# First key weights over ScalarE's DMA queue, centred first and last tiles, row scales on ScalarE, and new orders in a four-layer attention kernel

## The chip, the cores and the metric

The kernel runs on one core of one Trainium2 chip. The metric is the device time of one execution in microseconds, given as the median of several runs. The profile shows one execution: PE is TensorE, DVE is VectorE, ACT is ScalarE, POOL is GpSimd, SP is SyncE, which here issues DMAs only.

## The reference

Four layers follow each other on one sequence of 2048 tokens and 512 features, in 32 heads of 16: linear attention (A), sliding-window attention (B, a window of 256 keys), A and B again with the same weights. Each layer adds its result to x.

```python
phi = lambda t: jnp.where(t > 0, t + 1, jnp.exp(t)) + 1e-6
# A, on q, k, v of the normalised x
pq, pk = phi(q), phi(k)
kv = jnp.einsum("bhsd,bhse->bhde", pk, v)
z = jnp.einsum("bhsd->bhd", pk)
num = jnp.einsum("bhqd,bhde->bhqe", pq, kv)
den = jnp.einsum("bhqd,bhd->bhq", pq, z)[..., None] + 1e-6
o = num / den
# B
scores = jnp.einsum("bhqd,bhkd->bhqk", q, k) * (Dh ** -0.5)
mask = (idx[:, None] - idx[None, :] >= 0) & (idx[:, None] - idx[None, :] < W)
p = _softmax(jnp.where(mask[None, None], scores, -1e9), axis=-1)
o = jnp.einsum("bhqk,bhkd->bhqd", p, v)
# the model; _A_ref and _B_ref end with the product with wo
x = A_x
x = x + _A_ref(_layernorm(x, axis=-1), A_wqkv, A_wo)
x = x + _B_ref(_layernorm(x, axis=-1), B_wqkv, B_wo)
x = x + _A_ref(_layernorm(x, axis=-1), A_wqkv, A_wo)
x = x + _B_ref(_layernorm(x, axis=-1), B_wqkv, B_wo)
```

## The kernel before

The sequence is cut into 16 tiles of 128 tokens. All weights and activations stay in the core's memory in bf16.

**Layer one, keys.** For each tile VectorE takes the mean and variance (`stats` L377, `aggr` L378), a small addition and GpSimd's power give the reciprocal deviation `rs` (L382, L383), VectorE writes the normalised tile `xn` (L384). It is transposed: the first five tiles by PE (L398) with an eviction (L405), the rest by DMA transposes on SP (L392). From the transposed tile in `XQ` PE forms k (`tok`, L423) with the key weights `wA[:, :, 512:1024]`; `phi` turns k into the positive feature: ScalarE's exponential `E` (L447), VectorE's minimum `E1` (L450), then one of two forms. In the plain form VectorE takes the maximum with k + 1 straight from PSUM (`phi`, L454). In the other, called near in the code, ScalarE writes k + 1 (`R`, L449) and VectorE takes the maximum of two bf16 tiles (`mx`, L452). The Gram products `g` (L527) collect xnᵀ·phi(k) in four banks of PSUM over all tiles. The q of two tiles at a time (L483) goes through the same `phi`; `BY_ACT` lists the tiles of q that take the form with `R`.

**Barrier one.** From the Gram matrix follow kv and z (L542, L551), the matrix M = kv·wo (L581), the denominators (L597), their reciprocals (L606), their spread over features (L616) and the scaling of q (L626, L628). The layer's output is one product with M for each tile (`aout`, L423) and an addition to x (L641).

**Layer two** runs tile by tile: norm, transposes, q and k (`feat`, L437), v (`bv`, L423, evicted to `vS`, L410), small DMAs that lay keys and values out (L673, L692), scores (L713, L749, L829), exponentials on ScalarE (L723, L758, L838; 156 of them), masks (L731, L763, and on GpSimd L809), the product with v (L859), the division (L871, L872), the output product `bout` (L423), and x's update. The norm and the keys of layer three (`a_k`, `a_v`) follow for each tile; its key-value sums (L506) close **barrier two**, which is built like the first. **Layer four** repeats layer two with the output DMAs at its end (L915, L981).

**The start.** Nine matmuls on zeros (L1124) and up to seven fillers (`FILL`, L277) run on PE before the first data. SP issues x and the key weights in two halves in turn. ScalarE's queue issues one small DMA at the start (L1119) whose only reader is a wait ahead of the first layout DMA.

**What sets the order.** Nothing is decided at run time. The program makes a list of operations; `TABLE` is a packed table with a place in the order, an engine and a PSUM bank for each. `place` unpacks it, `synchronise` works out the semaphore waits, and each engine plays its own operations in that order. An operation that waits holds up all behind it on its engine. SP's DMAs use a ring of 48 semaphores.

## Time and profile before

| what | value |
| --- | --- |
| median of 3 runs | 410.35 us |
| lowest and highest run | 409.96 and 411.26 us |
| the profiled execution, its own time | 409.59 us |
| its span, first to last instruction | 407.9 us |
| granted TensorE clock, mean | 0.996 |
| PE busy | 395.0 us, 97% of the span |
| ACT busy | 350.4 us, 86% |
| DVE busy | 348.3 us, 85% |
| POOL busy | 130.3 us, 32% |
| bytes moved by DMA | 37.14 MB, 91 GB/s over the span |

A row of the timeline gives the start, the length, the engine, the line, what is written and what is read, how often the instruction comes in a row, and in brackets the idle time ahead of it with what ended it. A row of a window gives its length, then the busy time of each engine with the number of its instructions, the granted clock, the DMA engines' share and their rate. In the table of groups the last figure is the idle time ahead of the group's instructions.

### The profile page before, as it was taken

How to read it: one execution, taken by the hardware profiler on the slowest of the kernel's cores; microseconds unless marked ns; L12 is line 12 of the kernel's file. 1: busy time of each engine (PE TensorE's matmuls, PEld its weight loads, DVE VectorE, ACT ScalarE, POOL GpSimd, SP SyncE). 2: the span in 40 equal slices, each digit the busy share in tenths (PEclk: the TensorE clock that was granted, in tenths of full speed). 3: DMA queues.
4: the chain of work that ended last, by engine and by line, in shares of the span. 5: the costliest groups of instructions: out<-in, count | busy, mean ns of one | idle time of the engine just before them, and what ended most of it. 6: DMA issues, size and time to landing. Idle time of an engine off the chain costs nothing.

```text
span 407.9 us, 16954 instructions
## 1 busy us (share of the span) xinstructions
PE 395.0 (97%) x7402; PEld 255.8 (63%) x7402; DVE 348.3 (85%) x816; ACT 350.4 (86%) x444; POOL 130.3 (32%) x222
## 2 busy tenths in 40 slices
PE   8999999999999999999999999999999989999996
PEld 3744676677475567565657767576657746666674
DVE  6998899999998899888879789998998688766675
ACT  3743669999999998999997378999999999989991
POOL 4678562030342342431302132121116052303421
PEclk9999999999999999999999999999999999989999
DMA  7566015652264423363222101353315443342442
GB/s 242 113 163 192 4 29 132 160 106 56 60 115 81 121 68 96 88 113 82 70 64 33 27 2 28 83 121 95 80 29 133 74 129 91 97 123 55 123 94 69
DMA packets 66609, 37.14 MB, mean 91 GB/s; under 512 B 47656, under 2 KB 61864, under 8 KB 66536
## 3 DMA queue, kind: packets, MB, share of 16 engines
q1 hardware_dynamic: 66048, 34.75, 36.7%
q8 instruction: 58, 0.95, 1.0%
q0 software_dynamic: 480, 1.31, 0.9%
q14 instruction: 15, 0.12, 0.1%
q10 hardware_dynamic: 8, 0.00, 0.0%
HBM read 6.29 MB, written 2.10 MB: 21 GB/s over the span
## 4 chain that ended last, share of the span: by engine, by line
PE 65%; ACT 25%; DVE 7%; issue 1%; POOL 0%; POOLq 0%
PE ps L423 23%; ACT pb L723 15%; PE ps L859 12%; PE ps L437 10%; PE ps L713 6%; PE ps L483 5%; ACT pb L838 4%; ACT vp L723 4%; PE ps L527 3%; PE ps L829 1%; DVE xres L641 1%; DVE XQ L628 1%; DVE stats L377 1%; PE ps L1124 1%; PE ps L506 1%
## 5 line engine op out<-in xcount | busy, mean ns | idle before, releaser
L723 ACT ACTIVATE pb<-ps 128x1024 bf16<-128x1024 f32 (+2 forms) x216 | 199.8, 1022 | 8.4 <-PE ps L713 7.1
L859 PEld LDWEIGHTS ps<-vB,pb 128*128 128x128 bf16 x2560 | 79.0, 96 | 12.0 <-issue 2.7
L859 PE MATMUL ps<-vB,pb 128*128 128x34 bf16 x2560 | 84.9, 177 | 1.2 <-issue 0.5
L437 PE MATMUL ps<-xT,wBp 128*128 128x128 bf16 x1024 | 69.9, 221 | 0.6 <-ACT pb L723 0.5
L809 POOL TENSOR_SCALAR_AFFINE_SELECT pb<-pb 128x1024 bf16<-128x1024 bf16 x34 | 39.5, 1161 | 91.2 <-DVE pb L731 28.0
L437 PEld LDWEIGHTS ps<-xT,wBp 128*128 128x128 bf16 x1024 | 59.5, 98 | 12.8 <-issue 5.1
L382 POOL TENSOR_SCALAR ve<-mv 128x1 f32<-128x1 f32 x63 | 17.5, 278 | 154.5 <-DVE mv L378 152.9
L447 ACT ACTIVATE tE<-ps 128x512 bf16<-128x512 f32 x64 | 38.2, 606 | 20.6 <-PE ps L423 11.7
L713 PE MATMUL ps<-XQ,kB 32*128 32x256 bf16 (+3 forms) x992 | 48.2, 269 | 2.8 <-ACT vp L723 0.5
L423 PE MATMUL ps<-wA,XQ 128*128 128x512 bf16 x192 | 48.8, 379 | 0.0
L641 DVE TENSOR_TENSOR xres<-ps,xres 128x512 bf16<-128x512 f32 x63 | 42.8, 684 | 5.0 <-PE ps L423 4.9
L731 DVE TENSOR_TENSOR pb<-pb,tri 128x512 bf16<-128x512 bf16 (+1 forms) x108 | 43.1, 407 | 4.6 <-ACT pb L723 4.3
L377 DVE BATCH_NORM_STATS2 stats<-xres 128x6 f32<-128x512 bf16 x64 | 43.2, 684 | 2.5 <-DMA xres<-in_A_x_dram 2.1
L838 ACT ACTIVATE pb<-ps 128x1024 bf16<-128x1024 f32 x42 | 41.2, 1054 | 0.5 <-PE ps L829 0.4
L383 POOL TENSOR_TENSOR rs<-ve,negh 128x1 f32<-128x1 f32 x64 | 37.9, 592 | 7.8 <-DVE ve L380 2.5
L423 PE MATMUL ps<-wBv,xT 128*128 128x512 bf16 x128 | 34.4, 381 | 0.5 <-ACT pb L838 0.5
L483 PE MATMUL ps<-XQ,wA 128*128 128x256 bf16 x256 | 34.2, 273 | 0.4 <-ACT pb L723 0.4
L423 PE MATMUL ps<-M,XQ 128*128 128x512 bf16 x128 | 33.5, 380 | 0.4 <-DVE XQ L628 0.2
L423 PE MATMUL ps<-wBo,oT 128*128 128x512 bf16 x124 | 33.0, 380 | 0.4 <-ACT pb L723 0.3
L713 PEld LDWEIGHTS ps<-XQ,kB 32*128 32x128 bf16 x992 | 14.8, 92 | 28.3 <-ACT pb L723 7.3
L871 DVE RECIPROCAL rc<-ps 128x16 f32<-128x16 f32 x64 | 16.0, 252 | 14.8 <-PE ps L859 13.7
L483 PEld LDWEIGHTS ps<-XQ,wA 128*128 128x128 bf16 x256 | 23.4, 98 | 7.9 <-ACT pb L723 0.9
(133 smaller groups left out, 556.1 us busy)
## 6 DMA issues: line engine op xcount, KB each, us to landing
vB<-vS SPq DMA_DIRECT2D x64, 136.0 KB, 2.5
kB<-vp SPq DMA_DIRECT2D x60, 128.0 KB, 2.1
out_dram<-xres POOLq DMA_DIRECT2D x10, 128.0 KB, 2.4
wA<-in_A_wqkv_dram SPq DMA_DIRECT2D x2, 512.0 KB, 5.5
xres<-in_A_x_dram SPq DMA_DIRECT2D x2, 512.0 KB, 5.3
pb<-in_B_wqkv_dram SPq DMA_DIRECT2D x1, 1024.0 KB, 6.1
xres<-in_A_x_dram SPq DMA_DIRECT2D x3, 256.0 KB, 4.6
out_dram<-xres SPq DMA_DIRECT2D x5, 128.0 KB, 2.8
```

The costliest lines, as they stand in the source:

```text
L377: self.on("DVE", "stats", lambda e: e.bn_stats(K.stats[:, t, :], x()), key, dve(512), rd=rd, wr=[("stats", t)], **held)
L423: m = e.matmul(K.ps(ps), lhs(c), rhs(c), start=c == 0 and not whole, stop=c == 3)
L437: m = e.matmul(K.ps(ps)[:, f * P:(f + 1) * P], w(c, f), xT(c), start=c == 0, stop=c == 3)
L447: self.on("ACT", "E", lambda e: e.activation(K.tE[:, s, :], K.ps(ps), ACT.Exp, bias=0.0), key, act(512), wr=[("tE", s)], ps=[ps])
L483: m = e.matmul(K.ps(ps)[:, 256 * h:256 * h + 256], K.wA[:, c, f * P:(f + 1) * P], xT(c), start=c == 0, stop=c == 3)
L641: self.on("DVE", "res", lambda e: e.tensor_tensor(K.xres[:, t, :], K.ps(po), K.xres[:, t, :], ALU.add), key, dve(512), rd=[("xres", t)], w ...
L713: m = e.matmul(K.ps(ps[gq])[:, ns * i:ns * i + ns], K.kB[rows, j % 4, 2 * f + b, :, :], K.XQ[rows, f, q:q + ns], start=True, stop=True, ti ...
L723: return e.activation(out(2 * h, 2, ns), i, ACT.Exp, bias=0.0, scale=0.25)
L731: return e.tensor_tensor(x, x, K.tri[:, 0, sh:64].unsqueeze(1).unsqueeze(1).to_broadcast([P, 4, n, 64 - sh]), ALU.mult)
L809: return e.affine_select(out=x, in_=x, compare_op=ALU.is_ge, fill=0.0, base=-2, pattern=[[0, 16], [-2, 64]], channel_multiplier=1)
L838: return e.activation(far(h), i, ACT.Exp, bias=0.0, scale=0.25)
L859: m = e.matmul(K.ps(ps)[:, 34 * u:34 * u + 34], K.P((b // 2) % rp)[:, gq, f, o:o + P], K.vB[:, (b // 2) % 4, b % 2, r, :], start=i == 0, s ...
```

## The change

1. **Key weights.** ScalarE's queue loads the two halves of layer one's key weights as its first instructions, each with a semaphore of its own; the first two k products wait for these. SP no longer loads them, and the small DMA with its wait is gone.
2. **First two tiles centred.** For tiles 0 and 1 of layer one (`CENTRED`), ScalarE writes mean − x (`xc`, an Identity with scale −1 and the mean as its bias), PE transposes that in two halves, and the halves are evicted with a factor of −1 into `xT`. The k product reads this centred tile, and ScalarE's `E` and `R` take the row scale `rs` as their factor. The normalised tile is still written for the Gram matrix. Since PE no longer transposes it, a DMA transpose on SP brings it to `XQ` for the q product: 13 such transposes in layer one instead of 11.
3. **Keys with `R`.** The keys of tiles 0 to 7 of layer one (`KEYS_BY_ACT`) take the form with `R` and `mx`, and so do q tiles 7 to 10 of layer one's q (`BY_ACT`).
4. **Last tile of layer two.** Its output product is formed in halves, as the program's last tile is already; its norm is centred as in 2; k and v of layer three read the centred tile, with the row scale in `E`, `R` and in v's eviction.
5. **New table.** All orders, the choice of engine where there is one, and the banks. PE keeps its number of instructions; ScalarE has 472 operations instead of 447; GpSimd issues 6 output DMAs instead of 10 and SP 9 instead of 5.

```diff
-BY_ACT = {2: (0, 1, 2, 3, 4, 5, 6), 3: (4, 5, 6, 7, 8)}
+BY_ACT = {2: (0, 1, 2, 3, 4, 5, 6, 7, 8, 9, 10), 3: (4, 5, 6, 7, 8)}
+CENTRED = (0, 1)
+KEYS_BY_ACT = (0, 1, 2, 3, 4, 5, 6, 7)
...
-        seq += [xs(0, 1), wk(0), wk(1), xs(1, 2), w("wAq", "wA", "A_wqkv", 0, 512), xs(2, 4), xs(4, 6), xs(6, 8), xs(8, 12)]
+        seq += [xs(0, 1), xs(1, 2), w("wAq", "wA", "A_wqkv", 0, 512), xs(2, 4), xs(4, 6), xs(6, 8), xs(8, 12)]
...
+        if centred is not None:
+            slot, col = centred
+            self.on("ACT", "xc", lambda e: e.activation(K.xn[:, slot, :], x(), ACT.Identity, bias=K.mv[:, t, 0:1], scale=-1.0), key + 0.015, act(512), rd=rd + [("mv", t)], wr=[("xn", slot)])
+            for h in range(2):
+                half = Tile(1, K.cls)
...
+                        m = e.transpose(K.bf(half, 256)[:, c * P:(c + 1) * P], K.xn[:, slot, (2 * h + c) * P:(2 * h + c + 1) * P], K.ident[:])
...
+                self.either("Te", lambda e, eng, h=h, half=half: e.activation(K.xT[:, col, 2 * h:2 * h + 2, :], K.bf(half, 256).rearrange("p (c n) -> p c n", c=2), ACT.Copy, scale=-1.0) if eng == "ACT" else
...
+            by_pe = False
...
+        scale = lambda: dict(scale=K.rs[:, row, :]) if row is not None else {}
...
+        self.on("ACT", "E", lambda e: e.activation(K.tE[:, s, :], K.ps(ps), ACT.Exp, bias=0.0, **scale()), key, act(512), rd=own, wr=[("tE", s)], ps=[ps])
+        if near or row is not None:
+            self.on("ACT", "R", lambda e: e.activation(out(), view(K.ps(ps)), ACT.Identity, bias=K.one[:], **scale()), key + 0.005, act(512), rd=[("one",)] + own, wr=wr, ps=[ps], after=after)
...
-            po = self.b_out(j, k, tail, j in WHOLE[ph])
+            po = self.b_out(j, k, tail, j in WHOLE[ph], ph == 2 and j == T - 1)
...
+                end = j == T - 1
+                col = 1 if end else None
+                self.norm(j, k, 3, lambda j=j: K.XQ[:, :, j * P:(j + 1) * P], [("XQ", j)], tail and not end, po, near=end, centred=(1, 1) if end else None)
+                self.a_k(j, k + par["k_ak"], col)
...
-            tsem, touched = cx.enter_context(nc.semaphore("s_touch")), []
+            ksem, half = [cx.enter_context(nc.semaphore(f"s_key{h}")) for h in range(2)], []
...
-                    e.dma_start(self.kB[0:1, 3, 0:4, :, :].rearrange("p k n a -> p k (n a)"), self.A_wqkv.rearrange("(k p) c -> p k c", p=P)[0:1, :, 0:128]).then_inc(tsem, 16)
+                    for h in range(2):
+                        e.dma_start(self.wA[:, 2 * h:2 * h + 2, 512:1024], self.A_wqkv.rearrange("(k p) c -> p k c", p=P)[:, 2 * h:2 * h + 2, 512:1024]).then_inc(ksem[h], 16)
...
-                    if o.name == "kd" and not touched:
-                        touched.append(1)
-                        e.wait_ge(tsem, 16)
+                    if o.name == "k" and len(half) < 2:
+                        e.wait_ge(ksem[len(half)], 16)
+                        half.append(o)
```

What the table's new numbers do is seen in the engines' lists. PE at the start, before (a row is a line of the program, the operation, output and inputs, shape, and how often it comes in a row; `kB` holds the zeros of the warm matmuls and fillers, `vp` the normalised tiles, `ident` the identity of a transpose):

```order
L1124 MATMUL ps<-kB 128x512 x9
L277 MATMUL ps<-kB 128x512 x4
L398 MATMUL ps<-ident,vp 128x128 x4
L277 MATMUL ps<-kB 128x512
L398 MATMUL ps<-ident,vp 128x128 x4
L277 MATMUL ps<-kB 128x512
L423 MATMUL ps<-wA,XQ 128x512 x4
```

And with the change, where the line numbers have moved (L280 is the filler, L393 a half transpose of a centred tile, L439 the k product, L506 the q product):

```order
L1159 MATMUL ps<-kB 128x512 x9
L393 MATMUL ps<-ident,xn 128x128 x2
L280 MATMUL ps<-kB 128x512
L393 MATMUL ps<-ident,xn 128x128 x2
L280 MATMUL ps<-kB 128x512
L439 MATMUL ps<-wA,xT 128x512 x6
L414 MATMUL ps<-ident,vp 128x128 x4
L439 MATMUL ps<-wA,xT 128x512 x2
L280 MATMUL ps<-kB 128x512 x2
L414 MATMUL ps<-ident,vp 128x128 x4
L439 MATMUL ps<-wA,XQ 128x512 x4
L506 MATMUL ps<-XQ,wA 128x256 x4
```

Single fillers now stand between the four pairs of half transposes (two of the pairs are left out above), two more stand behind the eight k products of the centred tiles, and the first q products come earlier in the list than the 24 in a row that followed the third tile's k before.

ScalarE at the start, before:

```order
L1119 DMA kB<-in_A_wqkv_dram 1x4x128
L405 ACT_TABLE_LOAD
L405 ACTIVATE XQ<-ps 128x4x128 x3
L447 ACTIVATE tE<-ps 128x512 x2
L405 ACTIVATE XQ<-ps 128x4x128
L447 ACTIVATE tE<-ps 128x512 x3
```

With the change (L386 is the centring, L397 the eviction of a half, L421 that of a whole transposed tile, L465 `E`, L467 `R`; `rs` among the inputs is the row scale):

```order
L1154 DMA wA<-in_A_wqkv_dram 128x2x512 x2
L386 ACT_TABLE_LOAD
L386 ACTIVATE xn<-xres,mv 128x512 x2
L397 ACTIVATE xT<-ps 128x256 x4
L465 ACTIVATE tE<-ps,rs 128x512
L421 ACTIVATE XQ<-ps 128x4x128
L467 ACTIVATE vp<-ps,one,rs 128x512
```

The two weight loads stand ahead of everything, two centrings and four half evictions ahead of the first exponential, and an `R` now follows each key's `E`.

VectorE behind the Gram matrix, ahead of layer two's first scores, before (L606 is the reciprocal of the denominators, L628 the scaling of q, L641 the update of x):

```order
L606 RECIPROCAL rec<-ps 128x128
L454 SCALAR_TENSOR_TENSOR XQ<-ps,tE 128x2x256
L641 TENSOR_TENSOR xres<-ps,xres 128x512 x2
L377 BN_STATS stats<-xres 128x6
L628 TENSOR_TENSOR XQ<-ps,XQ 128x4x128
```

With the change (L629, L651 and L664 are those three lines, L470 is `mx`):

```order
L629 RECIPROCAL rec<-ps 128x128
L377 BN_STATS stats<-xres 128x6
L468 TENSOR_SCALAR tE<-tE 128x512
L378 BN_AGGR mv<-stats 128x2
L470 TENSOR_TENSOR XQ<-XQ,tE 128x2x256
L651 TENSOR_TENSOR XQ<-ps,XQ 128x4x128 x3
```

The features of q come as `mx` on two bf16 tiles where they were the plain form from PSUM, and the updates of x and the scalings of q stand in another order.

171 lines of the change are left out of this document (92 added, 79 removed).

## The prediction

> **What bounds the kernel now.** I read the page first, then the chain of waits from start to end, then the timeline and the windows of the stretches that the change touches.
>
> ```profile
> span 407.9 us, 16954 instructions
> PE 395.0 (97%) x7402; PEld 255.8 (63%) x7402; DVE 348.3 (85%) x816; ACT 350.4 (86%) x444; POOL 130.3 (32%) x222
> ...
> PE 65%; ACT 25%; DVE 7%; issue 1%; POOL 0%; POOLq 0%
> ```
>
> PE is busy in 97% of the span, and 65% of the chain are its rows, so the stages differ only in who makes PE wait. The windows tell that (length, then busy time of PE, PEld, DVE, ACT, POOL):
>
> ```profile
> 7.50:25.00 17.50, 17.49 (x114) 10.34 (x115) 17.13 (x49) 13.25 (x24) 11.69 (x27) 1.00 0.72 196
> 25.00:45.50 20.50, 20.46 (x197) 10.38 (x196) 17.06 (x40) 6.46 (x11) 16.98 (x31) 1.00 0.43 114
> ...
> 49.10:60.00 10.90, 10.90 (x134) 7.55 (x131) 10.70 (x25) 7.01 (x12) 6.05 (x11) 1.00 0.12 27
> ...
> 70.00:105.00 35.00, 34.76 (x672) 23.45 (x672) 33.18 (x79) 33.92 (x40) 6.51 (x12) 1.00 0.44 98
> 105.00:134.00 29.00, 27.54 (x607) 17.69 (x607) 27.06 (x65) 28.62 (x34) 8.90 (x15) 1.00 0.50 95
> 134.00:226.00 92.00, 91.24 (x1814) 57.65 (x1811) 79.25 (x187) 85.80 (x105) 26.15 (x39) 1.00 0.37 81
> 226.00:262.00 36.00, 36.00 (x458) 24.09 (x455) 31.85 (x77) 26.00 (x43) 8.82 (x18) 1.00 0.14 32
> 262.00:400.00 138.00, 132.79 (x3169) 90.70 (x3167) 110.31 (x253) 133.79 (x159) 37.36 (x50) 0.99 0.40 95
> ```
>
> Layer one (7.5 to 45.5): PE full. Behind the Gram matrix (49 on) PE and VectorE are full together. Layer two: PE with 2.46 us without work (0.24 + 1.46 + 0.76), most of it between 105 and 134, where ScalarE is busy 28.62 of 29. Barrier two (226 to 262): PE with no idle time. Layer four: ScalarE, 133.79 of 138. The orders of PE and ScalarE in layer four are nearly those of before, so that stage is costed at nothing. PE's work as such hardly changes; so a gain can only come out of the start, of PE's idle time, and of bubbles inside its rows.
>
> **The change part by part.** The sum is made against the profiled execution, 409.59 us with 407.9 of span. It lies 0.76 below the median of 410.35; the differences are carried over to the median.
>
> *The start.* Three engines of the timeline:
>
> ```profile
> 1.25 4.02 PE L1124 MATMUL ps<-kB 128*128 128x512 bf16 x9 [1.25 <-DVE kB L1116]
> 5.06 1.53 PE L277 MATMUL ps<-kB 128*128 128x512 bf16 x4
> 6.43 0.39 PE L398 MATMUL ps<-ident,vp 128*128 128x128 bf16 x4
> ...
> 7.51 1.09 PE L423 MATMUL ps<-wA,XQ 128*128 128x512 bf16 x4
> ```
>
> ```profile
> 0.80 1.19 ACTq L1119 DMA_DIRECT2D kB<-in_A_wqkv_dram  x1
> ...
> 6.86 1.09 ACT L405 ACTIVATE XQ<-ps 128x512 bf16<-128x512 bf16 x2 [3.56 <-PE ps L398]
> ```
>
> ```profile
> 2.96 0.69 DVE L377 BATCH_NORM_STATS2 stats<-xres 128x6 f32<-128x512 bf16 x1 [1.77 <-DMA xres<-in_A_x_dram]
> ...
> 4.69 0.18 DVE L378 BATCH_NORM_AGGREGATE mv<-stats 128x2 f32<-128x6 f32 x1
> 4.81 0.41 DVE L384 TENSOR_SCALAR vp<-xres,mv,rs 128x512 bf16<-128x512 bf16 x1
> ```
>
> Before, the first normalised tile is ready at 5.22 (4.81 + 0.41); its transposes stand behind four fillers, at 6.43, and the first k product waits for the eviction, at 7.51. Now the first product needs a mean and no power. The second aggregate ends at 4.87. A centring is an Identity with a pointer, 0.69 (row below): the second centred tile is ready at 5.56. The warm matmuls end at 5.27; half transposes stand between single fillers, and half evictions follow on ScalarE, 0.40 each (two of 128 × 256 take 0.80 at the end of the kernel, row below). Three of them behind 5.56 give 6.8; the first k starts at 6.8 to 7.1, 0.4 to 0.7 earlier. But two fillers now stand behind the eighth k product, 0.43 (half of the 0.86 of four products of that shape, below), unless they fill a bubble that was there anyway: the first four products took 1.09. Bounds −0.7 and 0; I take −0.3.
>
> *Weights on ScalarE's queue.* The two halves leave at 0.80, beside the first x tiles, not behind them on SP.
>
> ```profile
> GB/s 242 113 163 192 4 29 132 160 106 56 60 115 81 121 68 96 88 113 82 70 64 33 27 2 28 83 121 95 80 29 133 74 129 91 97 123 55 123 94 69
> ```
>
> The first slice moved 242 GB/s. Two x tiles are 256 KB, 1.1 us at that rate; if they share it evenly with 512 KB of weights, they end 1.1 later. Bounds 0 and +1.1. In the row above the first reading of x stands 2.2 us behind its issue, so volume is the lesser part of it: +0.1. The Trainium skill speaks against this part: "DMA: Bandwidth & Descriptors", in its rules for kernel authors, says that spreading transfers over issuing engines gives no bandwidth, since all use the same 16 DMA engines, and saves only time at issue. By that rule the term would be the full 1.1; in no row of before are both queues at work on such loads, so the trace can't say.
>
> *Keys by ScalarE in layer one.* Groups of the first 60 us:
>
> ```profile
> L447 ACT ACTIVATE tE<-ps 128x512 bf16<-128x512 f32 x27 | 15.7, 598 | 13.5 <-PE ps L423 6.9 <-DVE vp L454 3.8 <-PE ps L483 2.3
> ...
> L454 DVE SCALAR_TENSOR_TENSOR vp<-ps,tE 128x512 bf16<-128x512 f32 x16 | 10.7, 676 | 0.1
> ...
> L449 ACT ACTIVATE XQ<-ps,one 128x512 bf16<-128x512 f32 x7 | 4.6, 691 | 0.1
> ...
> L452 DVE TENSOR_TENSOR XQ<-XQ,tE 128x512 bf16<-128x512 bf16 x7 | 2.9, 417 | 0.0
> ```
>
> Eight keys lose 676 ns on VectorE and gain 417 there: 8 × 0.26 = 2.1 us less; ScalarE gains 8 × 0.69 = 5.5. PE idles 0.05 us in these 38, so VectorE's relief can only close bubbles. Pieces of the chain:
>
> ```profile
> 7.51 1.09 PE ps L423 x4
> ...
> 13.42 0.86 PE ps L423 x4
> ...
> 17.98 1.29 PE ps L527 x6
> ...
> 26.19 1.46 PE ps L527 x6
> ```
>
> The same four k products take 1.09 and 0.86, six Gram products 1.46 and 1.29: 0.4 in two pieces. Bounds 0 and −0.8, twice that; I take −0.3. On the other side stands ScalarE: busy 13.25 of 17.5 up to 25 us, and six of the eight new operations fall there, 4.1. That leaves 0.15, so E of a later tile can come late. After 25 it has 14 us free, which bounds the delay to a tile or two: 0 to +1.0; I take +0.2. (The Trainium skill, "ScalarE: Activation LUTs", on what the table load costs, adds about 93 ns for each pointer operand; the rows, 691 with and 598 without, agree. Four operations with a row scale would be 0.4 more by it, in just this tight stretch.)
>
> *q of tiles 0 and 1* now reads DMA transposes in place of PE's.
>
> ```profile
> 4.84 5.82 SPq L294 DMA_DIRECT2D xres<-in_A_x_dram  x2
> 11.18 1.29 SPq L392 DMA_TRANSPOSE XQ<-vp  x1
> ```
>
> ```profile
> vB<-vS SPq DMA_DIRECT2D x64, 136.0 KB, 2.5
> ```
>
> SP is held to 10.66 by the wait before its last x load. Two transposes of 1.29, and 2.5 to land as for the transfer above, end at 15.7; if the wait ends earlier, with two loads less ahead of it, 1 to 2 us sooner. PE's new order reaches these q products at 14 to 15. Bounds 0 and +1.5; I take +0.2.
>
> *49 to 70.* Three q tiles change form on VectorE (−0.78), one eviction of a transposed tile comes over from ScalarE (a copy of that size took 0.42, below). ScalarE takes three of 0.69 and has 3.9 us free until 60. PE is full here, so the difference works on bubbles only. Bounds +0.4 (the copy alone) and −0.8; I take −0.3, near the net.
>
> *Layer two.* ScalarE gets one R, two evictions of v and one of a product more: 0.69 + 2 × 0.74 + 0.60 = 2.8 us.
>
> ```profile
> L410 ACT ACTIVATE vS<-ps 128x512 bf16<-128x512 f32 x3 | 2.2, 741 | 0.0
> L410 ACT ACTIVATE XQ<-ps 128x512 bf16<-128x512 f32 x2 | 1.2, 597 | 0.0
> ```
>
> Only the R stands early, at the fifth exponential; the product's eviction comes at the 85th of 156 and those of v behind the 130th, where PE leads and ScalarE has 6.2 us free (92.00 − 85.80): that time is the cover. Queued behind each of them are exponentials, and PE's products with v wait for those. Without cover +2.8, with all of it 0; I take +0.3. The new orders of PE and VectorE there work on the 2.46 us that PE idles; no row prices an order. Bounds −2.5 and, the same the other way, +2.5; I take −0.8, half of the 1.46 between 105 and 134, since VectorE, at 27.06 of 29, is unloaded of the same operations.
>
> *Last tile of layer two.* Its power and normalisation leave its path, but PE is busy 36.00 of 36.00 there: the stretch waits for PE and not for the norm. Bounds −1 and +1 (the latency of power and normalisation, either way); 0.
>
> *End.* Two output transfers more on SP, at its 0.41 each:
>
> ```profile
> 401.83 0.80 ACT L410 ACTIVATE oT<-ps 128x256 bf16<-128x256 bf16 x2 [2.90 <-PE ps L897]
> ```
>
> ```profile
> 402.05 0.42 DVE L405 COPY oT<-ps 128x512 bf16<-128x512 bf16 x1 [0.49 <-PE ps L398]
> ```
>
> ```profile
> 403.80 0.81 SPq L915 DMA_DIRECT2D out_dram<-xres  x2
> ```
>
> They stand ahead of the last two in one queue: 0 to +0.4; I take +0.1.
>
> Sum: −0.3 + 0.1 − 0.3 + 0.2 + 0.2 − 0.3 + 0.3 − 0.8 + 0 + 0.1 = −0.8. That is 408.8 for the profiled execution and 409.5 for the median.
>
> **The rivals.**
>
> B, *the orders close PE's gaps*: all 2.46 of layer two, not 0.8 of it (−1.7), the start by its full 0.7 (−0.4) and the bubbles of layer one by 0.8 (−0.5): 409.5 − 2.6 = 406.9. For it: PE's work does not grow, and VectorE, full from 7.5 to 25 and from 49 on, loses 2.5 us. Against: ScalarE, which leads in 105 to 134, loses nothing there.
>
> C, *ScalarE sets the end of layer two*: its four operations count in full, 2.8 in place of 0.3, and half of the orders' 0.8 is lost: 409.5 + 2.5 + 0.4 = 412.4. It decides if ScalarE leads from 105 through the last exponentials of layer two. For it: 28.62 of 29.00. Against: the 6.2 us behind 134.
>
> D, *the x tiles wait for the weights*: the second lands 1.1 later (+1.0 on the term taken), the fillers run out, and PE goes on at the pitch of its first row (4.02 / 9 = 0.45, against 0.22) for some eight matmuls, +1.8: 409.5 + 2.8 = 412.3. It decides if the second x tile's reading starts after 4.7. Against: the 2.2 us of the first row, mostly latency. The Trainium skill's rule above is this one's.
>
> E, *it doesn't do what it says*: the start is earlier, but PE then waits at the next tile, and nothing is left: 410.0 to 410.6, inside A's own range.
>
> **How the numbers follow.** A change smaller than 0.3%, 1.23 us, can't be told from none. A (409.5, own range 408.2 to 410.7, E in it) has 0.42, of which 0.17 lies below 409.12 and 0.01 above 411.58; B 0.27; C 0.21; D 0.10. Faster 0.17 + 0.27 = 0.44; slower 0.01 + 0.29 (C and D less 0.02 that end short of the bound) = 0.30; same the rest, 0.26. The range goes a microsecond below B, for what the new order may close in layer four's 5.2 idle us of PE, and 0.4 above C: 405.9 to 412.8.
>
> **What would show it.** Right: the first k at 6.8 to 7.1; PE without idle time to 45; VectorE's busy time to 45 down by some 2 us and ScalarE's up by some 6; PE's idle time in layer two near 1.7 us; layer four as long as it was. Wrong: a first reading of x later than 3.2 (D); a gap of PE ahead of a q product before 20 us with a DMA as releaser; ScalarE without idle time behind 134 (C); PE without idle time from 70 to 226 (B). And it falls if layer four, whose first tiles come out of the new order of barrier two, changes its length by more than 1 us: the trace of before has no row for that.

## The result, and the profile after

The changed kernel is slower: 414.43 us median of 5 runs (413.51 to 417.12) against 411.03 for the kernel before in the same set (409.96 to 412.12, 5 runs), a ratio of 1.0114 with a 95% interval of 1.0088 to 1.0139. In a second set it took 415.98 us (412.59 to 417.56, 4 runs) against 410.29 (13 runs), 1.0127 [1.0064, 1.0191]. The forecast was 409.5 us, in a range that ended at 412.8.

The page of the changed kernel, in the lines that answer those of before:

```profile
span 414.7 us, 16990 instructions
PE 395.4 (95%) x7402; PEld 255.3 (62%) x7402; DVE 342.0 (82%) x816; ACT 363.0 (88%) x468; POOL 127.4 (31%) x214
...
PE 39%; ACT 23%; DMA 4%; issue 3%; DVE 2%; POOL 0%; POOLq 0%; SPq 0%; DVEq 0%
```

PE's work is what it was (395.4 us, 395.0 before), in a span that is 6.8 us longer. VectorE lost 6.3 us of work and ScalarE gained 12.6, as the change meant. New in the chain is DMA, with 4%: PE now waits for transfers. (This execution is the slowest of the five, 417.12 us.) The windows of the changed kernel:

```profile
7.50:25.00 17.50, 16.94 (x111) 9.61 (x108) 17.18 (x55) 15.66 (x29) 12.69 (x30) 1.00 0.76 183
25.00:45.50 20.50, 20.46 (x175) 10.48 (x174) 15.47 (x37) 9.02 (x17) 17.14 (x30) 1.00 0.47 123
49.10:60.00 10.90, 10.72 (x117) 7.05 (x116) 10.63 (x26) 7.94 (x15) 4.30 (x8) 1.00 0.10 23
70.00:105.00 35.00, 34.70 (x706) 24.05 (x698) 32.17 (x77) 33.95 (x41) 6.17 (x10) 1.00 0.41 87
105.00:134.00 29.00, 26.97 (x563) 16.59 (x562) 26.86 (x65) 28.50 (x34) 9.57 (x17) 1.00 0.46 90
134.00:136.00 2.00, 0.46 (x3) 0.25 (x4) 1.03 (x4) 1.71 (x2) 0.00 (x0) 1.00 0.81 43
136.00:138.00 2.00, 2.00 (x33) 0.83 (x32) 1.03 (x2) 0.50 (x1) 0.00 (x0) 0.52 0.73 172
138.00:140.00 2.00, 2.00 (x73) 1.93 (x69) 0.85 (x4) 1.44 (x2) 0.79 (x2) 0.62 0.00 0
134.00:226.00 92.00, 89.34 (x1765) 56.27 (x1766) 74.93 (x177) 85.17 (x101) 25.60 (x37) 0.98 0.40 81
226.00:262.00 36.00, 35.11 (x482) 24.32 (x481) 29.90 (x76) 25.91 (x49) 8.73 (x17) 1.00 0.13 19
262.00:400.00 138.00, 131.34 (x3028) 87.60 (x3026) 110.79 (x256) 134.70 (x156) 34.64 (x47) 1.00 0.42 96
```

Read the small windows first. From 134 to 136 PE worked 0.46 of 2 us, and behind that its granted clock is 0.52 and 0.62: it pays once for the idle time and again for the clock. ScalarE has less to do behind 134 than before (85.17 of 92, 85.80 before), so it isn't the bound there. In layer one PE now has 0.56 us idle up to 25, where it had 0.01.

The start and the first stall, on VectorE, PE and SP's queue of the changed kernel:

```profile
3.40 0.69 DVE L377 BATCH_NORM_STATS2 stats<-xres 128x6 f32<-128x512 bf16 x1 [2.21 <-DMA xres<-in_A_x_dram]
...
5.28 0.69 DVE L377 BATCH_NORM_STATS2 stats<-xres 128x6 f32<-128x512 bf16 x1 [0.97 <-DMA xres<-in_A_x_dram]
```

```profile
7.00 0.28 PE L393 MATMUL ps<-ident,xn 128*128 128x128 bf16 x2 [1.06 <-ACT xn L386]
...
8.00 1.46 PE L439 MATMUL ps<-wA,xT 128*128 128x512 bf16 x6
...
24.72 1.04 PE L439 MATMUL ps<-wA,XQ 128*128 128x512 bf16 x4 [0.56 <-DMA XQ<-vp]
```

```profile
16.68 0.58 SPq L300 DMA_DIRECT2D pb<-in_B_wqkv_dram  x1
17.31 6.56 SPq L408 DMA_TRANSPOSE XQ<-vp  x2
```

The first reading of x is 0.44 later than before's 2.96, and the second stands at 5.28; the first k product is 0.5 later (8.00, 7.51 before). At 24.72 PE waits for a transpose that was issued 0.63 us behind the 1 MB load of layer two's weights.

The stall in layer two, on PE and on SP's queue of the changed kernel, then SP's queue of the kernel before at the same place:

```profile
133.24 0.40 PE L736 MATMUL ps<-XQ,kB 32*128 32x256 bf16 x8
135.54 1.35 PE L439 MATMUL ps<-wBo,oT 128*128 128x512 bf16 x4 [1.91 <-DMA oT<-o]
```

```profile
127.20 1.19 SPq L408 DMA_TRANSPOSE xT<-xn  x1
128.43 1.36 SPq L696 DMA_DIRECT2D kB<-vp  x1
129.90 0.53 SPq L715 DMA_DIRECT2D vB<-vS  x1
130.47 1.30 SPq L408 DMA_TRANSPOSE oT<-o  x1
```

```profile
126.35 1.02 SPq L673 DMA_DIRECT2D kB<-vp  x1
127.55 1.19 SPq L392 DMA_TRANSPOSE oT<-o  x1
```

The output product of tile 5 reads a transpose issued at 130.47, the fourth DMA within 3.3 us. By the semaphore events it landed at 135.41, after 4.93 us; before, it was issued ahead of the vB load and landed 2.35 us later. The second profile of the changed kernel has the same place, and worse:

```profile
136.21 1.49 PE L439 MATMUL ps<-wBo,oT 128*128 128x512 bf16 x3 [2.66 <-DMA oT<-o]
```

This trace lacks the first of the four matmuls. The transpose landed at 135.70 there, so the wait was nearer 2.2 us. The windows from 136 to 142 are granted half clock:

```profile
136.00:138.00 2.00, 1.79 (x11) 0.44 (x10) 0.26 (x1) 0.00 (x0) 0.00 (x0) 0.50 0.80 186
138.00:140.00 2.00, 2.00 (x50) 1.83 (x43) 1.40 (x4) 1.70 (x2) 0.46 (x2) 0.50 0.00 0
140.00:142.00 2.00, 2.00 (x63) 1.87 (x60) 1.34 (x4) 1.06 (x2) 0.33 (x1) 0.50 0.04 8
```

The 312 exponentials of layers two and four serve as milestones. The table gives how much later than in the profile of the kernel before an exponential starts (starts counted from the span's start; the 157th is the first of layer four). Each row is one execution, and not always a typical one: that of `only_queue` ends 2.13 later, though its kernel's median is that of before, and that of `keys_on_sp` took 412.39 us where its kernel's median is 416.49. So a difference under about 2 us means little here, and the medians decide:

```
kernel           1st   65th   73rd  145th  153rd  161st  265th   last
after          +2.33  +2.81  +5.25  +5.73  +7.04  +6.03  +5.64  +6.87
again          +1.64  +2.74  +6.67  +7.47  +8.64  +7.63  +6.86  +8.05
keys_on_sp     +2.60  +3.09  +2.83  +2.86  +3.10  +2.09  +1.80  +2.89
only_queue     +1.75  +2.36  +2.38  +2.17  +2.17  +2.08  +1.38  +2.13
only_r         +5.16  +6.86  +6.81  +6.71  +6.71  +6.63  +6.68  +7.41
only_last      +0.80  +0.75  +0.80  +0.73  +0.73  +3.91  +2.74  +2.91
parts_only     +6.74  +8.26  +9.83  +9.69  +9.69 +13.68 +12.65 +12.79
order_only     +9.01  +9.93  +9.67  +9.85 +11.05 +21.07 +20.50 +21.36
early_before   +0.18  +2.23  +1.98  +2.25  +2.49  +1.47  +0.96  +2.88
late_before    +2.48  +4.09  +4.13  +3.93  +3.93  +3.84  +2.67  +2.97
keys_plain     +2.87  +3.42  +3.15  +3.19  +4.27  +3.25  +2.78  +4.30
product_later  +1.98  +2.47  +3.96  +6.06  +7.10  +6.07  +5.40  +7.11
swap_vb        +2.01  +4.79  +4.48  +4.52  +5.73  +4.71  +3.82  +4.95
load_later     +2.50  +2.99  +3.01  +3.05  +4.39  +3.36  +2.58  +4.41
repaired       +1.88  +2.36  +2.10  +3.46  +3.70  +2.68  +2.17  +2.80
repaired_l4    +2.03  +2.56  +2.30  +2.42  +3.98  +2.96  +2.04  +3.24
early_l4       +0.81  +2.88  +2.61  +2.65  +3.57  +2.56  +2.04  +3.43
bridge         +0.06  +0.24  +0.18  -0.02  +1.11  +2.51  +1.17  +1.21
```

Two questions follow: which stretch loses the time, and whether the parts or the orders are to blame.

### The profile page after: what moved, and what is told of

The parts are those of the page before. It is cut to its first block, busy times and chain, and to the rows that moved or that the text cites. A ratio compares the mean times of both kernels' runs of the same rounds, so it can differ in the third digit from the quotient of the medians.

```text
span 414.7 us, 16990 instructions
## 1 busy us (share of the span) xinstructions
PE 395.4 (95%) x7402; PEld 255.3 (62%) x7402; DVE 342.0 (82%) x816; ACT 363.0 (88%) x468; POOL 127.4 (31%) x214
## 4 chain that ended last, share of the span: by engine, by line
PE 39%; ACT 23%; DMA 4%; issue 3%; DVE 2%; POOL 0%; POOLq 0%; SPq 0%; DVEq 0%
ACT pb L746 14%; PE ps L439 12%; PE ps L882 9%; PE ps L453 6%; PE ps L736 5%; ACT pb L861 4%; ACT vp L746 3%; PE ps L506 2%; DMA oT<-o 2%; DMA vB<-vS 1%; PE ps L529 1%; DMA XQ<-xn 1%; PE ps L852 1%; ACT tE L465 1%; DVE XQ L651 1%
## 5 line engine op out<-in xcount | busy, mean ns | idle before, releaser
L832 POOL TENSOR_SCALAR_AFFINE_SELECT pb<-pb 128x1024 bf16<-128x1024 bf16 x33 | 38.4, 1165 | 95.6 <-DVE pb L754 41.1
L382 POOL TENSOR_SCALAR ve<-mv 128x1 f32<-128x1 f32 x62 | 18.7, 301 | 153.5 <-DVE mv L378 151.4
L664 DVE TENSOR_TENSOR xres<-ps,xres 128x512 bf16<-128x512 f32 x63 | 43.0, 684 | 9.5 <-PE ps L439 8.6
L465 ACT ACTIVATE tE<-ps 128x512 bf16<-128x512 f32 x61 | 36.6, 608 | 13.4 <-DVE vp L472 4.7
L439 PE MATMUL ps<-wA,XQ 128*128 128x512 bf16 x176 | 45.5, 379 | 0.8 <-DMA XQ<-vp 0.6
L439 PE MATMUL ps<-wBv,xT 128*128 128x512 bf16 x128 | 34.7, 381 | 0.7 <-ACT pb L861 0.5
L439 PE MATMUL ps<-wBo,oT 128*128 128x512 bf16 x120 | 32.2, 383 | 2.8 <-DMA oT<-o 2.8
L506 PE MATMUL ps<-XQ,wA 128*128 128x256 bf16 x256 | 34.1, 273 | 0.5 <-ACT pb L746 0.3
L439 PE MATMUL ps<-M,XQ 128*128 128x512 bf16 x128 | 34.2, 380 | 0.5 <-DVE XQ L651 0.2
L506 PEld LDWEIGHTS ps<-XQ,wA 128*128 128x128 bf16 x256 | 23.4, 98 | 8.6 <-issue 0.6
```

Source lines behind the costliest of these rows:

```text
L439: m = e.matmul(K.ps(ps), lhs(c), rhs(c), start=c == 0 and not whole, stop=c == 3)
L465: self.on("ACT", "E", lambda e: e.activation(K.tE[:, s, :], K.ps(ps), ACT.Exp, bias=0.0, **scale()), key, act(512), rd=own, wr=[("tE", s)] ...
L506: m = e.matmul(K.ps(ps)[:, 256 * h:256 * h + 256], K.wA[:, c, f * P:(f + 1) * P], xT(c), start=c == 0, stop=c == 3)
L664: self.on("DVE", "res", lambda e: e.tensor_tensor(K.xres[:, t, :], K.ps(po), K.xres[:, t, :], ALU.add), key, dve(512), rd=[("xres", t)], w ...
```

## The experiments

### The change again, and its start

**The same kernel once more.**

No edit.

> The changed kernel once more, unchanged. Its first profile shows the first exponential of layer two 2.3 us late against before, 3.2 us more lost between the 52nd and the 76th exponential, where PE waits 4.9 us for a DMA transpose of oT, and 1.5 us more up to layer four. Theory (lasting loss at the start, the middle part a matter of that execution's DMA): the first 1.8 to 2.3 us are there again, the loss at the transpose is under 1 us, ratio to before 1.008 to 1.013. Rival (the order itself places the product too close behind its transpose): the 3 us between the 52nd and 76th exponential are there again.

Measured: 1.0127 [1.0064, 1.0191]. The stall at tile 5 and the half clock behind it are there again (quoted above). But they don't come with every execution. Both profiles are of the slowest execution of their set (417.12 and 417.56 us). Five of the kernels below have the same DMAs in the same order at this place (`keys_on_sp`, `keys_plain`, `load_later`, `early_before`, `product_later`), and in their profiles the same transpose landed after 2.56, 3.44, 3.37, 2.50 and 2.92 us. PE's product in three of them, `keys_plain`, `load_later` and `early_before`:

```profile
134.54 1.04 PE L439 MATMUL ps<-wBo,oT 128*128 128x512 bf16 x4 [0.30 <-ACT pb L746]
...
134.41 1.02 PE L439 MATMUL ps<-wBo,oT 128*128 128x512 bf16 x4 [0.59 <-DMA oT<-o]
...
133.36 1.04 PE L439 MATMUL ps<-wBo,oT 128*128 128x512 bf16 x4 [0.30 <-ACT pb L746]
```

The execution with the median time of the first set, 414.43 us, had a granted clock of 1.000, where 3.4 us at half clock would make it 0.996. So this stall, with its half clock, goes with the slow executions of the change; it isn't what makes the median 1.1% longer.

**Key weights on SP again, the rest as changed.** The two halves leave ScalarE's queue and stand in SP's list behind the loads x2 and x4.

```diff
-                    for h in range(2):
-                        e.dma_start(self.wA[:, 2 * h:2 * h + 2, 512:1024], self.A_wqkv.rearrange("(k p) c -> p k c", p=P)[:, 2 * h:2 * h + 2, 512:1024]).then_inc(ksem[h], 16)
...
+                        if o.name in ("x2", "x4"):
+                            h = 0 if o.name == "x2" else 1
+                            e.dma_start(self.wA[:, 2 * h:2 * h + 2, 512:1024], self.A_wqkv.rearrange("(k p) c -> p k c", p=P)[:, 2 * h:2 * h + 2, 512:1024]).then_inc(ksem[h], 16)
```

> The changed kernel with the two key-weight loads back on SP's queue, behind the loads of x2 and x4 as before; all else as in the change. Theory Q (the weights on ScalarE's queue take the DMA engines from the first x tiles): the first two readings of x go back from 3.40 and 5.28 to about 2.96 and 3.98, the first k product starts at about 7.2 in place of 8.00, and 0.8 to 1.3 us of the time come back. Rival P (the start is late because of the order of PE and ScalarE): readings come earlier, but the k product not by more than 0.3, and the time changes by less than 0.4 us. Rival W (the weights were the last to come): the first k product gets later, 8.5 or more.

Measured: 416.49 us, 1.0148 [1.0098, 1.0198]. The first k product starts at 7.16, as theory Q had it, and none of the time comes back.

**Only the weights on ScalarE's queue, all else as before.**

```diff
-CENTRED = (0, 1)
-KEYS_BY_ACT = (0, 1, 2, 3, 4, 5, 6, 7)
+CENTRED = ()
+KEYS_BY_ACT = ()
...
-            po = self.b_out(j, k, tail, j in WHOLE[ph], ph == 2 and j == T - 1)
+            po = self.b_out(j, k, tail, j in WHOLE[ph])
...
-                end = j == T - 1
+                end = False
```

Before's `BY_ACT` and before's order go with it.

> The kernel before with one part alone: the key weights by ScalarE's queue at the start, in place of the small DMA and the two loads on SP; orders and all else of before. Theory Q: readings of x late by 0.4 and 1.3 us as in the changed kernel, first k product at 8.0 or later, 0.5 to 1.3 us slower than before. Rival P: readings later, but hidden by the four fillers ahead of the first transposes; within 0.4 us of before. A gain of more than 0.4 us would say that the weights were what the first k waited for.

Measured: 410.08 us (10 runs), 0.9997 [0.9972, 1.0022]. The first two readings of x, with the weights on SP and then with only the queue changed:

```profile
2.94 0.69 DVE L377 BATCH_NORM_STATS2 stats<-xres 128x6 f32<-128x512 bf16 x1 [1.75 <-DMA xres<-in_A_x_dram]
...
3.77 0.66 DVE L377 BATCH_NORM_STATS2 stats<-xres 128x6 f32<-128x512 bf16 x1
```

```profile
3.43 0.69 DVE L377 BATCH_NORM_STATS2 stats<-xres 128x6 f32<-128x512 bf16 x1 [2.24 <-DMA xres<-in_A_x_dram]
...
4.55 0.69 DVE L377 BATCH_NORM_STATS2 stats<-xres 128x6 f32<-128x512 bf16 x1
```

Against the kernel before (2.96 and 3.98) the second queue alone delays these readings by 0.5 and 0.6 us; in the changed kernel it delays the second by 1.5 (3.77 to 5.28). The Trainium skill, "DMA: Bandwidth & Descriptors", in its rules for kernel authors, says that loads spread over issuing engines share the same 16 DMA engines and gain no bandwidth; the readings agree. But the time doesn't follow them: alone the queue costs nothing that can be measured, and without it the change is as slow.

### Single parts in before's order

**`R` and `mx` for keys 0 to 7 and q tiles 7 to 10.**

```diff
-CENTRED = (0, 1)
+CENTRED = ()
...
-                end = j == T - 1
+                end = False
```

The output product in halves is undone too; weights on SP, before's order, each `R` right behind its `E`.

> The kernel before with one part alone: R and mx for the keys of tiles 0 to 7 and for q tiles 7 to 10; each R stands right behind its exponential on ScalarE, mx where the plain form stood, everything else in before's order. Theory (ScalarE has room: 13.25 of 17.5 us busy up to 25 us, 6.46 of 20.5 up to 45): VectorE loses 3 us of work and ScalarE gains 8; within 0.5 us of before, layer one not longer. Rival (ScalarE becomes the bound of the first 25 us, and R delays E): PE shows gaps with ScalarE as releaser before 25 us and the time rises by 1 us or more.

Measured: 416.63 us, 1.0156 [1.0107, 1.0205]. VectorE, ScalarE and PE of this kernel in layer one:

```profile
13.97 0.76 DVE L470 TENSOR_TENSOR vp<-vp,tE 128x512 bf16<-128x512 bf16 x2 [2.72 <-ACT vp L467]
...
16.20 0.41 DVE L400 TENSOR_SCALAR vp<-xres,mv,rs 128x512 bf16<-128x512 bf16 x1
```

```profile
12.67 1.27 ACT L467 ACTIVATE vp<-ps,one 128x512 bf16<-128x512 f32 x2 [0.42 <-POOL one L315]
```

```profile
16.66 0.40 PE L414 MATMUL ps<-ident,vp 128*128 128x128 bf16 x4 [1.56 <-DVE vp L400]
```

This is how a cheaper form costs time. `mx` saves VectorE 0.26 us, but it needs `R`, and VectorE stands 2.72 us in front of it. The normalisations queued behind `mx` (L400) are late, and PE waits for one of them. 0.42 of that is the constant tile of ones, which before's order writes later than this form needs it. Whether another place for `R` in that order would cost less was not tried.

**The last tile of layer two alone, in before's order.**

```diff
-CENTRED = (0, 1)
-KEYS_BY_ACT = (0, 1, 2, 3, 4, 5, 6, 7)
+CENTRED = ()
+KEYS_BY_ACT = ()
```

Before's `BY_ACT` and order, weights on SP.

> The kernel before, in its order, with the last tile of layer two alone as the change has it (first half of the projection from a half transpose, the tile centred by ScalarE, its row scale in the exponential, R and the value's eviction). Theory (the parts are cheap and the order around them costs): the time within 0.5 us of before, 410.5 to 411.5, a ratio of 0.998 to 1.003. Rival (the parts lengthen the chain at the barrier between layers two and three; where before's order and parts ran ahead of layer two, the change's last tile added 1.9 us between the exponentials 264 and 280): 412 to 413.5, a ratio of 1.004 to 1.008. A gain of the last tile alone would be 409 to 410, by the vector instructions that it takes off the chain.

Measured: 412.96 us, 1.0076 [1.0046, 1.0107]: the rival. PE in barrier two, where it had no idle time before:

```profile
235.70 0.40 PE L393 MATMUL ps<-ident,xn 128*128 128x128 bf16 x4 [1.30 <-ACT xn L386]
236.57 1.04 PE L439 MATMUL ps<-wA,XQ 128*128 128x512 bf16 x4 [0.47 <-DVE xT L398]
...
240.55 1.06 PE L529 MATMUL ps<-vp 128*128 128x129 bf16 x12 [0.51 <-ACT vp L426]
...
242.85 0.40 PE L414 MATMUL ps<-ident,oT 128*128 128x128 bf16 x4 [0.36 <-DVE zs L597]
```

These four gaps come to 2.64 us, the exponentials behind them to +3.2 (the 161st less the 153rd).

**Plain keys in the change.** The changed kernel with the plain form for keys 2 to 7.

```diff
-KEYS_BY_ACT = (0, 1, 2, 3, 4, 5, 6, 7)
+KEYS_BY_ACT = ()
```

> The changed kernel with one part undone: the keys of tiles 2 to 7 take the plain form on VectorE again where mx stood, and ScalarE loses six R (4.1 us); the centred tiles keep theirs; orders of the change, a few banks moved. Theory K (ScalarE's keys are what delays layer one): the first exponential of layer two comes 0.8 us or more earlier than in the change (61.3 or less) and the time falls by 0.8 to 2 us. Rival (VectorE needs the relief): first exponential later than 62.8 and the time longer by 1 us or more. Rival (neither): within 0.5 us of the change.

Measured: 416.54 us, 1.0172 [1.0147, 1.0198]. This fits the rival by which VectorE needs the relief in the new order (the first exponential is at +2.87), but the interval overlaps that of the change's second set, so it isn't shown; in before's order the same form costs.

### Parts or orders

**All parts, before's order; and the change's order without its parts.**

The first is the changed code with each new operation at the place, in before's table, of the one that it replaces. The second is the code of before with each operation at its counterpart's place in the change's table:

```diff
-CENTRED = (0, 1)
-KEYS_BY_ACT = (0, 1, 2, 3, 4, 5, 6, 7)
+CENTRED = ()
+KEYS_BY_ACT = ()
...
-                end = j == T - 1
+                end = False
```

> All parts of the change (weights on ScalarE's queue, centred tiles, R and mx for the early keys and the four late q tiles, the last tile of layer two) with before's order of the work; each new operation stands where the one that it replaces stood. Theory (the new orders are needed by the parts and give most of it back, but not all): slower than the change, 415 to 418.5, a ratio of 1.012 to 1.02, since R and mx alone in before's order came to 1.0156 and the last tile alone to 1.0076. Rival (the orders are what costs, the parts are cheap): under 413.5, a ratio under 1.008.

> The order of the change with none of its parts: before's forms of all operations and the key weights on SyncE's queue, each operation where its counterpart stands in the change's order (25 of the 2,570 operations a few places later, for want of a PSUM bank). Theory (the order carries the late transposes that cost most): slower than before by 3 to 6 us, 413 to 417, a ratio of 1.007 to 1.016, with the idle before the product of tile 5 at about 135 and the one in layer four at 364 to 368. Prediction's own term (the new orders are worth 0.8 us by themselves): 409 to 410.3. If the waits at 135 and 365 are there and nothing else is, 412 to 413.5.

Measured: parts alone 420.94 us, 1.0259 [1.022, 1.0297]; order alone 432.77 us, 1.054 [1.0497, 1.0583]. Together they are 1.0114 to 1.0127. So neither is good by itself: the parts cost 2.6% (10.6 us of 410), and the new order, made for them, takes back about half, 1.3 to 1.5%. Both kernels are slower than the ranges expected of them (415 to 418.5 and 413 to 417). Without its parts the order loses 9.0 us by the first exponential and 10.0 more in barrier two (+11.05 to +21.07), the two stretches that were written for centred tiles. The windows of the two kernels in layer one, parts alone first:

```profile
7.50:25.00 17.50, 13.95 (x81) 7.87 (x81) 11.83 (x37) 12.72 (x23) 7.53 (x21) 0.90 0.52 142
```

```profile
7.50:25.00 17.50, 12.84 (x86) 7.34 (x88) 14.06 (x41) 9.18 (x16) 9.54 (x25) 1.00 0.61 175
```

In neither is any engine full. PE, VectorE and ScalarE wait for each other in turn, which no sum of busy times shows.

**Before's layer one with the change behind it, and the reverse.** One kernel has before's parts and order up to the first exponential and the change's behind it, the other the reverse.

The table is put together from the two at the first exponential of layer two; in the first the diff above but for the last tile goes with it, in the second the last tile's lines alone.

> Two halves joined at the first exponential of layer two: up to it orders, engines and parts of before (weights on SP, no centred first tiles, plain keys, q 7 to 10 plain), behind it those of the change (its last tile of layer two included). Theory L (about 2 us of the loss lie in layer one and its barrier, the rest behind a late transpose in layer two): the first exponential is within 0.7 of before's 60.5; the time lies 0 to 2.5 us above before, and runs that show a granted clock of 0.996 or less are 3 us above those with 1.0. Rival (the loss is all in layer two and later): 4 us above before. Rival (all of it is early): equal to before.

> The other way round: up to the first exponential of layer two the change (weights on ScalarE's queue, centred tiles, keys and q with R), behind it before's orders and its whole last tile. Theory L: the first exponential 1.2 to 2.4 us later than in before, the product behind the late transpose of oT stands where before had it, so the time lies 1.5 to 2.5 us above before. Rival (all of the loss is in layer two and later): equal to before. Rival (all of it is early): 4 to 5 us above before.

Measured: 413.8 us, 1.0107 [1.0086, 1.0128]; 412.62 us, 1.0089 [1.0065, 1.0112]. Each half costs about 1% alone, and both together little more, so the two losses don't add. But the seams cost too, since the two orders differ there in what has been done: PE has a wait of 0.74 us at 66.8 in the first and of 1.13 at 66.5 in the second, and between the 1st and the 65th exponential the two lose 2.05 and 1.61 us, where the change itself loses 0.48 and 1.10. So a good part of each half's loss may be the seam's. The runs of the first don't go by the clock, as its theory had it: 413.19 us at 0.996, 413.58 and 414.07 at 1.000.

### Single late transposes

**The product of tile 5 later.** PE's two rows of that product are moved some 2.3 us down its order.

```diff
-L439 MATMUL ps<-wBo,oT 128x512 x4
...
+L439 MATMUL ps<-wBo,oT 128x512 x4
```

> The changed kernel with one operation moved: tile 5's output product in layer two stands behind the next two pieces of the product with v and eight feat products on PE, about 2.3 us later, so that the transpose of oT issued at 130.5 has 5.4 us in place of 3.1 ahead of it. Theory D (the product stands too close behind its transpose; PE then idles 1.9 to 2.7 us and the granted clock falls to one half for 3.4 us or 6.8 us): that wait is gone or under 0.4 us, no stretch of half clock between 130 and 145 us, and the median falls by 1.5 to 3.5 us against the change. Rival (the wait goes to the next product or to the keys of tile 5): the same loss 2 to 8 us later, and the time within 0.7 us of the change.

Measured: 416.13 us, 1.0184 [1.0159, 1.0209]. PE waits three times elsewhere: the two times below, and 0.88 us at 138.39 for VectorE's x (`xres`):

```profile
134.50 0.40 PE L736 MATMUL ps<-XQ,kB 32*128 32x256 bf16 x8 [1.22 <-ACT pb L746]
...
141.62 1.04 PE L439 MATMUL ps<-wBv,xT 128*128 128x512 bf16 x4 [1.04 <-DVE vp L688]
```

But the late transpose didn't occur in this execution: it landed at 133.44, after 2.92 us, before PE would have come to the product at its old place (133.64 in the change). So the profile doesn't say whether moving the product would have hidden it. The ratio is above that of the change's first set by its interval, and overlaps that of the second, so the later product is no gain.

**The transpose earlier.** On SP's queue it goes ahead of the vB load:

```diff
 L696 DMA kB<-vp 64x1024
+L408 DMA_TRANSPOSE oT<-o 128x4x128
 L715 DMA vB<-vS 128x1x544
-L408 DMA_TRANSPOSE oT<-o 128x4x128
```

> The changed kernel with one pair exchanged in SyncE's list: the transpose of o for tile 5 of layer two is issued ahead of the 128x1x544 vB load that stood before it. Theory (transposes that are issued close behind other DMAs land late, and the product of tile 5 is where TensorE pays for it): the transpose is issued 0.6 us earlier and lands in 2.4 to 4 us instead of 4.9 to 5.2, so by 134 instead of 135.4; the idle of 1.4 to 2.7 us before that product falls under 1 us, the half clock of 3.4 to 6.8 us behind it (1.7 to 3.4 us of lost work) is gone, and the time is 411.5 to 413.5, a ratio of 1.002 to 1.008. Rival (the stage is full on every engine, so that the wait only moves, as it did when the product was put later): no idle there, but waits of the same sum within the next 10 us, the time 414.5 to 416.5, a ratio over 1.010.

Measured: 414.08 us (10 runs), 1.008 [1.0056, 1.0105]. The transpose landed in 3.38 us, and PE's wait is the small one for ScalarE that stood there before the change (0.30):

```profile
135.86 1.04 PE L439 MATMUL ps<-wBo,oT 128*128 128x512 bf16 x4 [0.29 <-ACT pb L746]
```

The time is on the edge between the two theories (1.008), and the interval overlaps that of the change. In the trace the loss between the 65th and the 73rd exponential, 2.4 to 3.9 us in the two profiles of the change (5.25 − 2.81 and 6.67 − 2.74), is not there (4.48 − 4.79). But neither is it in `keys_on_sp`, `keys_plain`, `load_later` and `early_before`, where the transpose was not moved; there it landed after 2.5 to 3.4 us, and in the four profiles with the exchange after 2.4 to 3.4. Whether the exchange prevents the late landing is not shown.

**The 1 MB load behind the next transpose.**

```diff
-L300 DMA pb<-in_B_wqkv_dram
 L408 DMA_TRANSPOSE XQ<-vp 128x4x128
+L300 DMA pb<-in_B_wqkv_dram
```

> The changed kernel with the 1 MB load wBn moved behind the next transpose of XQ on SyncE's queue. Theory (that transpose lands in 7.1 to 7.4 us because it runs against the load, and the first k product behind it costs TensorE 1.0 to 1.5 us): it lands in 3 to 4 us, the idle at 24.7 goes, and the first exponential stands 0.7 to 1.2 us earlier, the time 413.3 to 415. Rival (VectorE, busy 17.2 of 17.5 us there, is the bound, and the wait for the transpose is only the one seen): the idle at 24.7 is replaced by one with a VectorE releaser, the first exponential within 0.4 us of the change's, the time 414.4 to 416.

Measured: 414.1 us, 1.0088 [1.0053, 1.0122]. The wait at 24.7 is gone:

```profile
24.39 1.03 PE L439 MATMUL ps<-wA,XQ 128*128 128x512 bf16 x4
```

but the first exponential is as late as in the change (+2.50, +2.33 there). So nothing shows that this wait was on the path, and that the time is lower than the change's can't be told from chance. It is also the time of the kernel with the exchange at tile 5 (414.08, in the same set), which this one doesn't have.

**Both, and one eviction in barrier one back on ScalarE.**

To the two diffs above comes, from VectorE's list to ScalarE's:

```diff
-L421 CAST xT<-ps 128x512
+L421 ACTIVATE xT<-ps 128x512
```

> The changed kernel with both exchanges (the 1 MB load behind a transpose, the transpose of o for tile 5 ahead of the vB load) and the eviction of the xT transpose in the barrier back on ScalarE, where before had it. Theory (the loss is the sum of single late operations in the new order, 1 to 1.5 us in layer one and the barrier and 3 to 4.5 us at tile 5): 410 to 412.5, a ratio of 0.999 to 1.006. Rival (the parts themselves make ScalarE and VectorE too full, so that each mended wait comes back at the next operation): 413.5 to 416, a ratio over 1.008.

Measured: 413.81 us, 1.0081 [1.0056, 1.0107]. The three together give what each exchange had by itself. PE's wait at that eviction in barrier one, 0.18 us for VectorE in the change, is 0.35 for ScalarE here.

**The same for a transpose in layer four**, in the repaired kernel and in the one with before's layer one (there with the exchange at tile 5 too):

```diff
+L408 DMA_TRANSPOSE oT<-o 128x4x128
 L715 DMA vB<-vS 128x1x544
 L696 DMA kB<-vp 64x1024
-L408 DMA_TRANSPOSE oT<-o 128x4x128
```

> The repaired kernel, and in layer four the transpose of o ahead of a vB and a kB load on SyncE's queue. Theory: that transpose lands near 362 instead of 364.5, the idle of 1.0 to 1.8 us before its product goes, and the time falls by 0.7 to 1.5 us against the repaired kernel's 413.8, to 412.3 to 413.1, a ratio of 1.004 to 1.007. Rival (the two loads that are now later cost the s products behind them as much, or the wait only moves): 413.5 to 414.5, a ratio over 1.0075.

> Before's parts and order up to the first exponential, the change's behind it, with both transposes of o (tile 5 of layer two, the one in layer four) ahead of the loads that stood before them. Theory (single late transposes carry the loss behind layer one): 1 to 1.8 us under the same kernel without the two exchanges (413.8), so 412 to 412.8, a ratio of 1.006 to 1.009, and the profile's span within 2 us of before's. If the rest of the change were worth the 0.8 us that the prediction gave to the orders, it would be 409.5 to 411. Rival (the wait moves on): 413.3 to 414.3.

Measured: 413.96 us, 1.008 [1.0038, 1.0122], and 414.0 us, 1.009 [1.0062, 1.0119]. The transpose is issued at 359.49 in the first and landed 2.29 us later, and the wait before its product, 0.77 us in the repaired kernel and 1.29 in the other, is gone in both; the times didn't move. In layer four ScalarE is busy 134.70 of 138 us in the change, so PE's wait there was probably covered.

### The last tile with its own order

The kernel before, with the change's last tile and its order from the 152nd to the 182nd exponential, before's order and forms elsewhere. At both seams the two orders have done the same operations. The edit is that of the last tile alone, with the change's numbers for 400 of its 2,577 operations in the table.

> The kernel before, with the change's last tile of layer two and the change's order only for the stretch around the barrier between layers two and three (from the 152nd to the 182nd exponential); ahead of it and behind it before's parts and order, and the two orders have done the same operations at both seams. Theory (parts and order gain only together, and this is the one place where the change gains: 1.0 us between the exponentials 152 and 160 in every run with both, of which 0.6 us go back before 168): 0.2 to 1.0 us under before, a ratio of 0.997 to 1.000, against 1.0076 for the same parts in before's order. Rival (the last tile costs with its order too, and the gain seen was made up for by what ran late ahead of it): 410.5 to 412, a ratio of 1.001 to 1.005.

Measured: 411.91 us (12 runs), 1.0058 [1.003, 1.0087]: the rival. PE as the last tile's work begins:

```profile
222.99 0.24 PE L736 MATMUL ps<-XQ,kB 32*128 32x64 bf16 x8 [0.39 <-DVE XQ L472]
...
225.09 0.29 PE L736 MATMUL ps<-XQ,kB 32*128 32x128 bf16 x8 [1.16 <-DVE o L895]
```

With nothing late ahead of it the stretch from the 145th to the 161st exponential is 2.5 us longer than before's. In the kernels that came late to it, it is from 0.8 shorter to 0.5 longer; that the other engines catch up there while PE waits is argued from this, not shown. With the change's order in all of layer two (before's layer one ahead of it) the 161st exponential came a microsecond earlier than here, +1.47 against +2.51, so the seam, or what the order does earlier, has a share that stays open. No version that ran beats the kernel before.

## Why the prediction was wrong, point by point

**The step that failed is the pricing of the sum's terms, of the parts as well as of the orders ("I take −0.8")**: it took an order to be worth part of the idle time that it might close, and the parts to be worth their durations on engines with time to spare, and added these. By that sum the parts come to 0 and the order to −0.8. Measured, the parts in the old order come to +2.6% (10.6 us). Run alone, the `R` of the keys and q tiles gives 1.56%, the last tile 0.76% and the queue −0.03%; the centred first tiles were not run alone. The new order takes 1.3 to 1.5% of it back, and 1.1 to 1.3% are left, while the same order without the parts costs 5.4%. So neither kind of term has a price of its own that could be added. No term was large by its durations; where the loss was followed, at the `R` and at the last tile, it is waiting in queues that run in order.

- *Start, −0.3.* The first k product came at 8.00 in place of 6.8 to 7.1 (7.16 with the weights on SP). The second x tile was read at 5.28, past the 4.7 that rival D had named.
- *Weights, +0.1.* D's mechanism was there: the second reading of x is 1.3 us later than before (5.28, 3.98), more than the full 1.1 that the sum did not take. Its price was not: clock 1.00, and a ratio of 0.9997 alone.
- *Keys by `R`, −0.3 and +0.2.* The moves in busy time came nearly as written: up to 45.5 VectorE 1.5 us less, ScalarE 5.0 more. What was left out is that `mx` waits for ScalarE, with the normalisations behind it on VectorE. The term is mis-sized by far: +1.56% in before's order, with the q tiles' `R` in it.
- *q of tiles 0 and 1, +0.2.* No gap before 20. But a transpose stood right behind the 1 MB load, and the wait came at 24.72 at a k product; moving the load took the wait away and brought the first exponential no earlier.
- *49 to 70, −0.3.* PE gained no time: 0.18 us of idle in 49.1 to 60, none before. That idle time is the wait at the copied eviction, under half of the copy's bound of +0.4, and it was there on ScalarE, too, when the copy went back (0.35).
- *Layer two's ScalarE work, +0.3, and rival C.* C's time, 412.4, is the nearest of the five, by a mechanism that did not happen: ScalarE had 6.8 us idle behind 134. The late transpose of tile 5, in this execution, was in no rival. PE idled 4.99 us from 70 to 226 (0.30 + 2.03 + 2.66), where 1.7 was forecast.
- *Last tile, 0.* PE was full there, and it was taken that a chain of other engines could not matter. It costs 0.76% in before's order and 0.58% with its own, though part of the second may be the seam's.
- *End, +0.1.* Nothing: the last exponential is 6.87 us later than before, the end of the span 6.8.
- *Layer four.* From its first exponential, the 157th (+5.89), to the last (+6.87) the change loses 0.98 us, and 0.55 in its second profile: within the 1 us that was forecast, but only just.

What stays open: the 1.1 to 1.3% that are left were not traced to single waits. The late transpose at tile 5 costs 2.4 and 3.9 us in the executions that have it, but it was in two of seven profiles with its order, so it doesn't account for the median. The three kernels that keep the whole change but for the exchange at tile 5 and other moved operations come to a ratio of 1.008 each; the change comes to 1.0114 and 1.0127, and the kernel with the load alone moved to 1.0088, with intervals that overlap. So the exchange may be worth a third of the loss, but that isn't shown. Each half of the change loses about 1% alone, with its seam in it. Some of the loss lies outside the span: the time beside it is 1.7 to 1.9 us in the runs of before, 1.7 to 3.0 in the first five of the change, and 1.7 to 1.8 in the four of its second set. The cause of that was not tried.

## What to carry to other kernels

Where every engine plays a fixed order, price a change by what stands behind each new wait in its queue, not by durations against idle time; a form that saved an engine 0.26 us here kept it waiting 2.7 us for its input. Parts and their order are one thing: each alone was worse here than both, so a part can't be judged in the old order, nor an order without its parts. And before a wait is mended, see whether it is there in more executions than the one profiled: the most striking stall of this case was in two of seven, each the slowest execution of its set, and what was moved on account of it gave nothing that can be told from chance.
